# Another issue sequence for the 3155 pieces of a DeltaNet and FNet kernel on one core

## Chip, core and metric

One core of one Trainium2 chip runs the whole kernel. The metric is the device time of one launch in microseconds (us). The engines are PE (TensorE, matmuls), PEld (the same engine's weight loads), DVE (VectorE), ACT (ScalarE), POOL (GpSimd) and SP (SyncE, which starts most DMAs).

## What is computed

```python
batch, n_heads, seq, head_dim = (4, 8, 768, 48)
def _attn_ref(q, k, v, beta):
    k_n = k / (np.linalg.norm(k, axis=-1, keepdims=True) + 1e-06)
    state = np.zeros((B, H, D, D), dtype=np.float32)
    for t in range(S):
        kt, vt, bt = (k_n[:, :, t], v[:, :, t], beta[:, :, t, None])
        y[:, :, t] = np.einsum('bhd,bhde->bhe', q[:, :, t], state)
        v_old = np.einsum('bhde,bhd->bhe', state, kt)
        state = state + bt[:, :, :, None] * np.einsum('bhd,bhe->bhde', kt, vt - v_old)
    ...
def _moe_ref(x, w_ch1, w_ch2):          # x: (4, 768, 384), the heads side by side
    mixed = np.real(np.fft.fft(np.fft.fft(x, axis=1), axis=2)).astype(np.float32)
    u = x + mixed
    mu = np.mean(u, axis=-1, keepdims=True)
    var = np.mean((u - mu) ** 2, axis=-1, keepdims=True)
    un = (u - mu) / np.sqrt(var + 1e-06)
    ch = np.maximum(un @ w_ch1, 0.0) @ w_ch2      # 384 -> 1536 -> 384
    return (u + ch).astype(np.float32)
```

The two weight matrices come as 64-bit floats and are made into 32-bit floats on the chip.

## The kernel before

**How the work is cut.** The recurrence is done in chunks. Each of the four batches b has six blocks T of 128 positions, so there are 24 units u (six per batch), and each unit holds 8 heads in four pairs. For a unit the kernel loads q, k and v, normalises k, turns q and k by matmuls against the identity (`turn`: the matmuls are `tr`, L357, and two evictions of 128x256 follow, by `copy`), forms the products of keys with keys and with queries (`keys`, `gram`, whose masked evictions are L581 and L596), and inverts a triangular matrix for each head and chunk on DVE (`invert`, pairs of instructions L871 and L876; the first units go by `invert16`, which begins with two wide transposes, L701, and uses a triangle of ones made by the memsets L2087 and L2089). `join`, `blocks` and `quarters` build larger inverses from smaller ones, `chain0` and `step` carry the state through the chunks, and `outputs` writes the rows of x for the block.

**The second half.** When the six blocks of a batch are there, DVE folds x for the Fourier transform (`turns`, L1339), PE multiplies by the tables (`seq`, `half_axis`), and `feat` adds x and takes mean and variance (L1499 to L1512). `normed` then makes the normalised rows of one block: its `apply` (L1525, tile pm, for batch 0 always on DVE) writes 128x384 values, PE turns them (L357, `pp<-pack,pm`, three matmuls), and evictions bring them back as rows R. There are three groups g of two blocks T for each batch. For a group, `mlp` runs six slices of the first layer (`first(i)`, L354, `pp<-R,w`, 128x256, twelve matmul records in the trace) with relu evictions, each followed later by its slice of the second layer (`second(i)`, L354, `pp<-w,R`, 128x384, eight records). Only the first batch uses the plain form `mlp`; the weights that it needs are made ready in 18 slices, each by six operations: ACT (L1931), DVE (L1934), ACT (L1937), DVE (L1942), POOL's addition (L1947) and DVE (L1950).

**What sets the order.** Every piece of work is recorded by `P.op(engines, fn, ...)` and gets a number. Nothing is issued then. At the end `P.issue` walks the text `ORDER` (L58 to L138): two characters are a piece's number, one more names the engine where the piece allows several (most evictions allow DVE or ACT, memsets DVE or POOL), one more gives a PSUM bank for every new bank, and for a paced DMA of SP two more name the piece after which it may start. Every engine executes its pieces in just this order, and waits for data by semaphores that the framework puts in. A number past the last piece is a fill: `fill(kind, bank)` issues matmuls whose result nobody reads (kind 3 is a pair of 64x64 by 64x256, kind 4 one of 128x128 by 128x256, L2159; kind 0, at the start, many small ones, L2153).

Of the kernel before, what the change touches and what calls it, by code (L numbers as in the profile page):

```python
# [57 lines left out]
ATAAAMDAPBAODAHDAEBACBxTCARAKBAZAZAaAPAYAbGEABALBAXASANDAFBAeFCA9APAcCAdCAhDAAfBAgCAiAJDA7APA+APADBA  # L58
8AOAjAlxWGBPHEBQCAkAUFAmAtAVApAuCxAOBRCxVCBSGFBTCAGDA-CBBBCAIDBACBUCAvBCEHAxDFAAAyBDCAwBECBVBGBWAWA1
BcAzBZBkA0A2BFFCBXBGxWEA3xWEBvBaBwDgAiDOAmxWEBJxWEBKBbArBzBHxWEBYB0BIxWEB3AoBjB4BgAnBMAqxWExWEBOBNBe  # L60
A4B7BpBhBLxWEB8A5BlBdBmB-BnCAxWEBoCyADCDC0CIAAjBqH-H-DGCFCECHC6C6BrCIIBA6BxxWGDhEDCLDiBDjCC7BHC8CCMD
XDXC9CByCPxXGDICB1CQBfB2CTBiB5DYGDDPBHCUB6CXB9CYDQCB+CbDaCCzCxWFDHCH4BECBDRCCcCCH3BeCfCFDZCxWFCgC5C5
DDCCGxXBxXFxWFH5C+EBDbGHxWFCjxWFxWFCJCkC1CAC-CH7DcCC3CIoC0CKxWFIPB8xWFDdCCnDACxWExWGCNAsCpDJAHxXDxXF
IQA4CoBtIRCOxWEDLCDyC2CIIDZDKCxWEDzCD2CIHB+ESCRD3HxWFICEUCCSEWCEXAEVCD0CD4CDwByD1CIJCqETCDSHCD5ECrCV
EYCD6xWBCWD7IDCZEZFEaDND3CaxWDD8D9DkAEIYCkCdDTCIKILEbEcIXD0CeAQDDWCNxWBITxWBH6DlCDUCEAHChIED-CD+CxWC
xWFEDCEECECCEBCCiBuxWADmCIZClEdxWGEFDxWGCmDCDzEGCEHCEICEgHxWGBsEJCENABEKEDH8H9EkCCsCuCtH+EhCFqEjCE+x
WFxWFIxCrCvEPCEfBEiCELCxWFFrCFDHEOCIvIZFCBEeCFBCFECFvGFsBEMCFACIwECEQCHCE-CERCFuBIFIGGYCGWElDGXCFFHF
HDMGaCEwFtCFwCEpCIMGbFFxEEyCEnCEzCHHGHFBEoCGcBFGGZCEtAFCwHGCFyFIHDCEmCIyElGdBEqHDHICIzIbFzI1EvCDEBFJ
I5FGExGEEsCErBE0F0DqBF1I0I6EOFKCI7FwFMHEuCE1CC4FQCI8GZINGeF4DF3BFOCF7CE5E7BFLBHEBGfFPCF5CI2E2IOFNCI3
# [2123 lines left out]
```

The heart of `P.issue` is this:

```python
            i = take(2)
            if i >= len(self.ops):
                fill(i - len(self.ops), take(1))
                continue
            o, self.ins = self.ops[i], None
            e = o.engs[0] if len(o.engs) == 1 else ENGINES[take(1)]
            for b in o.new:
                b.slot = take(1)
            after = take(2) if o.kb and e == "SP" else i
            o.fn(e)
```

The eviction helper, whose lines the profile shows for three kinds of instruction, reads:

```python
    def copy(e, o, i, scale=None):
        if e == "ACT":
            I(nc.scalar.activation(o, i, ACT.Copy, **({} if scale is None else {"scale": scale})))   # L363
        elif scale is None:
            I(eng(e).tensor_copy(o, i))                                                              # L365
        else:
            I(eng(e).tensor_scalar(o, i, scale, None, op0=ALU.mult))                                 # L367
```

## Time and profile before

| | before |
|---|---|
| median of 3 runs | 624.71 us (624.24 to 625.9) |
| the profiled execution: its own time | 624.21 us |
| its span | 622.4 us |
| mean granted TensorE clock | 0.997 |
| PE busy | 606.6 us (97%) |
| DVE busy | 542.3 us (87%) |
| ACT busy | 292.6 us (47%) |
| POOL busy | 28.7 us (5%) |

A share of busy time is a mean over stages with different limits: the first 147 us (the first units, the weights, and batch 0 up to its layers) look otherwise than the rest, so the views below are cut by stage. In a view by windows a row gives the window, its length, then for PE, PEld, DVE, ACT and POOL the busy time with the number of instructions, the granted clock, the share of DMA time and GB/s. In a timeline a row gives start, duration, engine, line, operation, output and inputs, shapes and count, and in brackets how long the engine was idle before it and what ended that.

### The profile page before, as it was taken

The numbers are of one execution on the slowest core, as the hardware profiler recorded it, in microseconds if no ns is written. First come the engines' busy times: TensorE is split into PE (matmuls) and PEld (weight loads), VectorE is DVE, ScalarE is ACT, GpSimd is POOL, SyncE is SP. The second block draws the span as 40 slices with busy tenths as digits, with TensorE's granted clock in tenths as the row PEclk, the third lists the DMA queues.
The fourth block names the chain that finished last, engine by engine and source line by source line (L and its number), as shares of the span: only waits on it lengthen the run. The fifth ranks groups of instructions, "written<-read, shape, count | busy, mean of one in ns | idle before, by whom it ended". The sixth has DMA issues, their size and how long they took to land.

```text
span 622.4 us, 23113 instructions
## 1 busy us (share of the span) xinstructions
PE 606.6 (97%) x9870; PEld 529.8 (85%) x9870; DVE 542.3 (87%) x1631; ACT 292.6 (47%) x903; POOL 28.7 (5%) x36
## 2 busy tenths in 40 slices
PE   8998899999999999999999999999999999999997
PEld 8787888776778877999898978898889899999997
DVE  6999899999989889999777999999977898967574
ACT  6999757464255542725446435446731113332220
POOL 2022410110000000000000000000000000000000
PEclk9999989999999999999999999999999999999999
DMA  9546544520023200200220220110000000000010
GB/s 196 159 110 176 148 108 106 137 68 19 14 70 69 54 19 1 75 18 1 66 54 16 41 56 10 26 52 16 4 29 3 2 2 25 2 1 1 26 52 25
DMA packets 85443, 32.01 MB, mean 51 GB/s; under 512 B 75996, under 2 KB 80829, under 8 KB 85341
## 3 DMA queue, kind: packets, MB, share of 16 engines
q1 hardware_dynamic: 85149, 30.31, 19.7%
q8 instruction: 77, 1.26, 0.8%
q10 hardware_dynamic: 192, 0.23, 0.2%
q14 instruction: 25, 0.20, 0.1%
HBM read 25.82 MB, written 4.72 MB: 49 GB/s over the span
## 4 chain that ended last, share of the span: by engine, by line
PE 79%; DVE 15%; issue 2%; DMA 1%; ACT 1%; SPq 0%; DVEq 0%; ACTq 0%
PE pp L354 73%; PE pp L2159 3%; PE pp L357 3%; DVE R L1339 2%; DVE tmp L871 2%; DVE w L1950 1%; DVE rr L876 1%; DVE eo L1339 1%; ACT us L363 1%; DVE pm L1339 1%; PE pp L2153 1%; DVE us L581 1%; DMA x<-in_moe_w_ch_dram 1%; DMA us<-in_v_dram 1%; DVE w L1934 1%
## 5 line engine op out<-in xcount | busy, mean ns | idle before, releaser
L354 PE MATMUL pp<-R,w 128*128 128x256 f32 (+1 forms) x832 | 181.5, 367 | 0.7 <-DVE R L581 0.6
L354 PEld LDWEIGHTS pp<-R,w 128*128 128x128 f32 x832 | 144.6, 190 | 19.8 <-DVE R L581 0.9
L363 ACT ACTIVATE us<-pp 32x128 f32<-32x128 f32 (+3 forms) x211 | 68.3, 351 | 61.2 <-PE pp L354 43.7
L354 PE MATMUL pp<-w,R 128*128 128x384 f32 (+1 forms) x288 | 91.0, 440 | 0.7 <-DVE w L1950 0.7
L354 PEld LDWEIGHTS pp<-w,R 128*128 128x128 f32 x288 | 51.8, 190 | 22.7 <-DVE w L1950 1.3
L354 PE MATMUL pp<-us 64*64 64x64 f32 (+4 forms) x2560 | 62.8, 229 | 1.5 <-ACT us L363 0.5
L354 PEld LDWEIGHTS pp<-us 64*64 64x64 f32 (+2 forms) x2560 | 53.3, 131 | 6.2 <-ACT us L363 2.6
L871 DVE TENSOR_TENSOR tmp<-rr 128x30 f32<-128x30 f32 (+13 forms) x150 | 50.9, 343 | 2.5
L876 DVE TENSOR_TENSOR rr<-rr,tmp 128x168 f32<-128x168 f32 (+11 forms) x150 | 48.8, 328 | 2.6
L354 PE MATMUL pp<-u,us 64*48 64x48 f32 (+2 forms) x1360 | 41.9, 218 | 1.6 <-DVE u L365 0.8
L354 PEld LDWEIGHTS pp<-u,us 64*64 64x64 f32 (+1 forms) x1360 | 35.9, 131 | 7.8 <-issue 3.5
L363 ACT ACTIVATE R<-pp 128x384 f32<-128x384 f32 (+10 forms) x69 | 26.8, 404 | 29.2 <-PE pp L354 16.3
L1772 DVE TENSOR_TENSOR us<-us,pp 128x256 f32<-128x256 f32 x64 | 26.1, 416 | 12.5 <-ACT us L363 8.2
L363 ACT ACTIVATE x<-pp 64x192 f32<-64x192 f32 (+1 forms) x69 | 21.5, 324 | 32.0 <-DVE u L1248 21.8
L363 ACT ACTIVATE u<-pp 64x192 f32<-64x192 f32 (+1 forms) x65 | 21.2, 325 | 29.3 <-PE pp L354 26.6
L354 PE MATMUL pp<-st,us 48*64 48x48 f32 (+1 forms) x1104 | 27.1, 222 | 3.3 <-issue 3.0
L1593 ACT ACTIVATE R<-pp 128x512 f32<-128x512 f32 x24 | 14.3, 595 | 33.8 <-PE pp L354 33.5
L1808 ACT ACTIVATE R<-pp 128x512 f32<-128x512 f32 x21 | 12.5, 597 | 34.2 <-PE pp L354 29.3
L354 PEld LDWEIGHTS pp<-st,us 48*64 48x64 f32 x1104 | 22.3, 134 | 6.7 <-issue 4.1
L354 PE MATMUL pp<-R,ws 128*128 128x192 f32 x144 | 28.0, 327 | 0.0
L354 PE MATMUL pp<-us,gd 128*128 128x192 f32 x144 | 27.6, 327 | 0.0
L363 ACT ACTIVATE us<-us,nr 128x48 f32<-128x48 f32 x112 | 26.7, 330 | 0.2 <-DVE nr L678 0.2
(214 smaller groups left out, 1170.6 us busy)
## 6 DMA issues: line engine op xcount, KB each, us to landing
out_dram<-x SPq DMA_DIRECT2D x11, 384.0 KB
us<-in_k_dram SPq DMA_DIRECT2D x16, 192.0 KB
us<-in_q_dram SPq DMA_DIRECT2D x16, 192.0 KB
us<-in_v_dram SPq DMA_DIRECT2D x16, 192.0 KB
x<-in_moe_w_ch_dram SPq DMA_DIRECT2D x11, 242.0 KB
R<-in_moe_w_ch_dram SPq DMA_DIRECT2D x8, 256.0 KB
ws<-in_moe_w_ch_dram SPq DMA_DIRECT2D x5, 242.0 KB
us<-in_q_dram SPq DMA_DIRECT2D x6, 181.5 KB
```

What stands on the lines that cost most here:

```text
L354: I(nc.tensor.matmul(o, lhsT=lhsT, rhs=rhs, start=start, stop=stop, skip_group_check=True))
L357: I(nc.tensor.matmul(o, lhsT=src, rhs=ident[p0:p0 + n, p0:p0 + n], is_transpose=True, start=start, stop=True, skip_group_check=True))
L363: I(nc.scalar.activation(o, i, ACT.Copy, **({} if scale is None else {"scale": scale})))
L581: I(nc.vector.tensor_tensor(z.LT.rearrange(hs, s=2)[:, s], bk()[:, 0], m_su[:, None, :].broadcast_to([128, NJ, 64]), op=ALU.mult))
L871: I(eng(e).tensor_tensor(T_, R[:, :, j + 1:32, j:j + 1].broadcast_to([128, ns, n, j]), R[:, :, j:j + 1, 0:j].broadcast_to([128, ns, n, j]) ...
L876: I(eng(e).tensor_tensor(R[:, :, j + 1:32, 0:j], R[:, :, j + 1:32, 0:j], T_, op=ALU.add))
L1339: I(eng(e).tensor_tensor(o, i0, i1, op=op))
L1593: I(nc.scalar.activation(o, s, ACT.Relu))
L1772: vec(256, lambda e: I(nc.vector.tensor_tensor(o, i0(), i1(), op=ALU.add)), [], [aH] + list(wr), pr - P.ev, use=n)
L1808: I(nc.scalar.activation(o, s, ACT.Relu))
L1934: I(eng(e).tensor_scalar(cc, cc, LB, UB, op0=ALU.max, op1=ALU.min))
L2159: I(nc.tensor.matmul(pst[bank][x, 0:256], lhsT=w[x, 0:128 // tiles], rhs=w[x, 0:256], start=True, stop=True, skip_group_check=True))
```

## The change

Only the text `ORDER` differs. The same 3155 pieces stand in it, in another sequence, with 47 fills as before (kind 0 once, kind 3 forty times; of kind 4 there are six where there were five, and the one of kind 2 is gone). 370 of the 397 choices of PSUM banks differ, and 167 of the anchors of paced DMAs. Where a piece may run on several engines, the choice differs for some: DVE has 1648 pieces where it had 1612, ACT 773 where it had 806, POOL 29 where it had 32. The pieces of PE stand in nearly the same order, mostly no more than 8 places away. Two of the 81 rows of the table, by way of example:

```diff
 ORDER = """
-ATAAAMDAPBAODAHDAEBACBxTCARAKBAZAZAaAPAYAbGEABALBAXASANDAFBAeFCA9APAcCAdCAhDAAfBAgCAiAJDA7APA+APADBA
...
+AKDAODARAPBAMDxTCAAATAIBAEBAZAPACBAbDEAdBASAaAPAeBGABAcCAhACAfCA9APAGDAgBAiBPDEAjAkAlAmA7AEAtAWBRBAU
...
```

The first place is the start of DVE's list. The names us_75 to us_80 are the buffers of the first six units, pp_61 to pp_68 the eight PSUM banks, w_73 from L2089 the triangle of ones, gd and rr the matrices that `invert16` works on. Before:

```order
L485 MEMSET us_79 128x8x16 x2
L2087 MEMSET w_73 128x256
...
L2089 MEMSET w_73 128x15
L485 MEMSET us_76 128x8x16
L365 COPY us_76<-pp_66 128x4x64
L485 MEMSET us_75 128x8x16
L540 SCALAR_TENSOR_TENSOR gd<-pp_64,pack,gd 128x8x32
L540 SCALAR_TENSOR_TENSOR gd<-pp_61,pack,gd 128x8x32
L1996 COPY bcol<-pp_66 128x6x4x8
L701 STREAM_TRANSPOSE rr<-gd 128x1024
```

And after:

```order
L485 MEMSET us_75 128x8x16
L365 COPY us_75<-pp_65 128x4x64
L365 COPY us_76<-pp_67 128x4x64
L540 SCALAR_TENSOR_TENSOR gd<-pp_61,pack,gd 128x8x32
L540 SCALAR_TENSOR_TENSOR gd<-pp_63,pack,gd 128x8x32
L365 COPY us_79<-pp_65 128x4x64
L2087 MEMSET w_73 128x256
...
L2089 MEMSET w_73 128x15
L365 COPY us_79<-pp_64 128x4x64
L1996 COPY bcol<-pp_62 128x6x4x8
L706 STREAM_TRANSPOSE nr<-bcol 128x32
L701 STREAM_TRANSPOSE rr<-gd 128x1024
```

Three evictions of turns (rows 5, 9 and 26) came from ACT to DVE, ahead of the first wide transpose L701, and the triangle moved from ahead of the first eviction to behind the keys' evictions L540.

The second place is DVE around the last of the two instructions L1525 of batch 0's second group, whose outputs PE turns (mv_110 is block T2, mv_111 block T3). Before, T3 comes at row 365 and T2, the later one, here:

```order
L1950 SCALAR_TENSOR_TENSOR w_73<-x_97,w_73 128x512
L871 TENSOR_TENSOR tmp<-rr 128x240
L876 TENSOR_TENSOR rr<-rr,tmp 128x15x16
L660 STREAM_TRANSPOSE nr<-bcol 128x32
L1512 RECIPROCAL mv_110<-mv_110 128x1
L1525 TENSOR_SCALAR pm_99<-x_96,mv_110 128x384
L871 TENSOR_TENSOR tmp<-rr 128x238
L876 TENSOR_TENSOR rr<-rr,tmp 128x14x17
L1950 SCALAR_TENSOR_TENSOR w_73<-ws,w_73 128x512
```

After, T2 comes at row 340 and T3, now the later one, here:

```order
L1950 SCALAR_TENSOR_TENSOR w_73<-x_97,w_73 128x512
L365 COPY R_98<-pp_64 128x512
L1503 BN_AGGR mv_112<-mv_112 128x2
L876 TENSOR_TENSOR rr<-rr,tmp 128x14x17
L871 TENSOR_TENSOR tmp<-rr 128x234
L365 COPY us_80<-pp_65 128x512
L876 TENSOR_TENSOR rr<-rr,tmp 128x13x18
L871 TENSOR_TENSOR tmp<-rr 128x228
L1525 TENSOR_SCALAR pm_99<-x_96,mv_111 128x384
L1950 SCALAR_TENSOR_TENSOR w_73<-ws,w_73 128x512
```

The later of the two stands 24 rows further down DVE's list, 399 where it was 375; the weights' step L1950 that followed it at a distance of three rows follows it at once.

The third place is PE where those transposes stand; rows that only repeat with other banks are left out. `pp<-pack,pm` are the transposes of a block, `pp<-R_81,w_72` a first layer, `pp<-w_73,R_81` a second layer, and the rows 64x2x64 the products of `gram`. Before, around the later block T2 (rows 1020 to 1060 of PE's list):

```order
L357 MATMUL pp_61<-pack,pm_99 128x128 x3
L354 MATMUL pp_68<-w_73,R_81 128x384
...
L354 MATMUL pp_64<-us_80 64x2x64
...
L354 MATMUL pp_63<-us_79 64x2x64
...
L354 MATMUL pp_67<-R_81,w_72 128x256 x6
L354 MATMUL pp_68<-w_73,R_81 128x384 x2
```

After, around the later block T3 (rows 1023 to 1063):

```order
L357 MATMUL pp_63<-pack,pm_99 128x128 x3
L354 MATMUL pp_61<-w_73,R_81 128x384
...
L354 MATMUL pp_65<-R_81,w_72 128x256 x6
...
L354 MATMUL pp_63<-us_80 64x2x64
...
L354 MATMUL pp_67<-us_79 64x2x64
...
L354 MATMUL pp_61<-w_73,R_81 128x384 x2
```

Behind the later block's transposes stand the same pieces, a second layer, two grams and the first layer of the new group, but the first layer now comes ahead of the grams.

160 lines of the change are left out of this document (80 added, 80 removed).

## The prediction

> **What bounds the kernel now.** I read the page first, then the engines' busy time by stage, then the timelines of PE and DVE where one stage hands over to the next, and last the waits of PE. The page's busy times, DVE's and ACT's 40 slices, and the chain that ended last:
>
> ```profile
> PE 606.6 (97%) x9870; PEld 529.8 (85%) x9870; DVE 542.3 (87%) x1631; ACT 292.6 (47%) x903; POOL 28.7 (5%) x36
> DVE  6999899999989889999777999999977898967574
> ACT  6999757464255542725446435446731113332220
> PE 79%; DVE 15%; issue 2%; DMA 1%; ACT 1%; SPq 0%; DVEq 0%; ACTq 0%
> ```
>
> PE holds 79% of the chain and DVE 15%. But DVE's digits are at 8 and 9 through the first third and ACT's only in the second to fourth slice, so the beginning has a limit of its own. The windows by stage show it; the last two rows cut the span in two:
>
> ```profile
> 0.00:8.90 8.90, 7.50 (x135) 6.71 (x136) 3.00 (x27) 3.82 (x10) 3.85 (x16) 1.00 0.88 179
> 8.90:42.00 33.10, 32.50 (x734) 25.62 (x735) 32.27 (x113) 31.78 (x105) 2.80 (x2) 1.00 0.59 154
> 42.00:87.00 45.00, 39.98 (x1387) 37.23 (x1385) 42.37 (x118) 34.50 (x113) 12.24 (x9) 0.96 0.55 143
> 87.00:106.00 19.00, 18.06 (x224) 16.62 (x223) 18.59 (x54) 13.59 (x43) 2.64 (x2) 1.00 0.45 109
> 106.00:137.74 31.74, 31.60 (x243) 24.34 (x241) 30.71 (x80) 17.40 (x42) 5.29 (x4) 1.00 0.43 105
> 147.30:500.00 352.70, 350.61 (x6223) 299.00 (x6223) 315.73 (x933) 159.51 (x504) 0.62 (x2) 1.00 0.13 31
> 0.00:147.30 147.30, 137.68 (x2799) 116.25 (x2799) 136.14 (x411) 104.79 (x320) 28.12 (x34) 0.99 0.52 128
> 147.30:622.40 475.10, 468.88 (x7073) 413.53 (x7072) 406.18 (x1221) 187.85 (x583) 0.62 (x2) 1.00 0.11 28
> ```
>
> From 8.9 to 137.74 us DVE is idle for 0.83, 2.63, 0.41 and 1.03 us (window less busy time), 4.90 in all: it is full. PE looks just as full there, but part of its work is fills, which nobody waits for. From 147.3 on PE is busy 350.61 of 352.70 us and DVE has 37 us of room. So work added to DVE ahead of 138 us moves the end, and work added behind 147 us doesn't. The handover shows in PE's timeline and, below it, in DVE's; the last two rows are POOL's:
>
> ```profile
> 137.89 0.52 PE L357 MATMUL pp<-pack,pm 128*128 128x128 f32 x3 [0.29 <-DVE pm L1525]
> 139.16 2.85 PE L354 MATMUL pp<-w,R 128*128 128x384 f32 x8 [0.75 <-DVE w L1950]
> 144.53 2.86 PE L354 MATMUL pp<-R,w 128*128 128x256 f32 x12 [0.61 <-DVE R L581]
> ...
> 131.50 1.39 DVE L871 TENSOR_TENSOR tmp<-rr 128x240 f32<-128x240 f32 x1
> 132.81 1.44 DVE L1525 TENSOR_SCALAR pm<-x,mv 128x384 f32<-128x384 f32 x1
> 136.22 0.40 DVE L871 TENSOR_TENSOR tmp<-rr 128x240 f32<-128x240 f32 x1
> 137.26 0.48 DVE L1525 TENSOR_SCALAR pm<-x,mv 128x384 f32<-128x384 f32 x1
> 138.42 0.69 DVE L1950 SCALAR_TENSOR_TENSOR w<-ws,w 128x512 int32<-128x512 int32 x1
> ...
> 131.28 1.34 POOL L1947 TENSOR_TENSOR w<-w,x 128x512 int32<-128x512 int32 x1 [14.00 <-DVE w L1942]
> 132.58 1.46 POOL L1947 TENSOR_TENSOR w<-w,ws 128x512 int32<-128x512 int32 x1
> ```
>
> PE's transposes start 0.15 us after the later L1525 (137.26 + 0.48 = 137.74), PE having been idle for 0.29 us. All that PE does in the next ten microseconds waits for DVE three times, 1.65 us in sum. I call the end of the later L1525 of this group the gate.
>
> **The change part by part.**
>
> *More rows on DVE ahead of the gate.* The gate is row 375 of DVE's list before and row 399 after: 24 instructions more, nearly all evictions that were ACT's. The price of one: the first five windows up to the gate hold 3.00 + 32.27 + 42.37 + 18.59 + 30.71 = 126.94 us in 27 + 113 + 118 + 54 + 80 = 392 instructions, counting the row 0 to 8.9, so 0.324 us. 24 x 0.324 = +7.8 us. The eviction itself costs more on DVE, so that 24 x 0.42 = +10.1 is the other end:
>
> ```profile
> L365 DVE COPY us<-pp 128x256 f32<-128x256 f32 x2 | 0.8, 421 | 3.4 <-PE pp L357 3.4
> L363 ACT ACTIVATE us<-pp 128x256 f32<-128x256 f32 x34 | 11.0, 402 | 3.1 <-PE pp L357 2.4 <-PE pp L354 0.6
> ```
>
> I take 7.8, since some of the new rows are small memsets and reciprocals.
>
> *The triangle moved behind the first evictions.* Its 16 memsets now lie in a time in which DVE is idle anyway:
>
> ```profile
> 1.69 0.27 DVE L2087 MEMSET w<- 128x256 f32 x1
> 2.03 0.29 DVE L2089 MEMSET w<- 128x1 f32 x15
> 5.84 0.42 DVE L365 COPY us<-pp 128x256 f32<-128x256 f32 x1 [3.38 <-PE pp L357]
> 8.01 0.88 DVE L540 SCALAR_TENSOR_TENSOR gd<-pp,pack,gd 128x256 f32<-128x256 f32 x2 [1.60 <-ACT gd L363]
> ```
>
> The 3.38 us ahead of the first eviction wait for PE's first turn, and no eviction can use them; the triangle could, and is taken out of them: +0.6 us (0.27 + 0.29, rounded up). Ends: 0, if DVE finds a later hole for it, and 0.6.
>
> *What takes the new work up.* DVE's hole of 1.60 us ahead of L540 is where the evictions at rows 5 and 6 now stand: 1.6 us, all of it used. The later holes sum to 4.90 us. They end on PE and ACT, and ACT's list is 29 rows shorter, so its results come earlier; ends 0 and 4.90, and I take half, 2.45. The gate then moves by 7.8 + 0.6 - 1.6 - 2.45 = +4.35 us, between +1.9 (all holes used) and +9.1 (24 dear evictions, no later hole used: 10.1 + 0.6 - 1.6).
>
> *Behind the gate.* PE was only 0.29 us ahead of DVE there, so PE follows the gate. Of the two waits behind it, the one on L1950 (0.75) shrinks, since that step stands one row behind the gate: L1950 then ends 0.69 us after the gate where PE, with its transposes, is ready after 0.15 + 0.52, and 0.1 is left. The one on the gram's eviction L581 (0.61) can go, since the first layer now comes ahead of the grams. -0.65 - 0.61 = -1.26; ends -1.36 and 0. The front: 4.35 - 1.26 = +3.1 us.
>
> *After 147 us.* PE's pieces are the same, in nearly the same order; other banks, anchors and engines set small waits. The longest waits of PE from 147.3 us on:
>
> ```profile
> PE pp L354 <- issue: 0.9, 1, 0.9
> PE pp L354 <- DVE st L1277: 0.4, 1, 0.4
> PE pp L354 <- DVE R L1339: 0.3, 1, 0.3
> PE pp L354 <- ACT us L363: 0.2, 1, 0.2
> ```
>
> Those on DVE and ACT sum to 0.9, and I let all three go: -0.9 us. The upper end of a gain is PE's whole idle time there, 475.10 - 468.88 = 6.22 us; on the other side new waits of the same size, +0.9. DMAs have room (share 0.11), POOL has two instructions there, and SP's queue is paced by anchors whose pieces come at nearly the same time: nothing for these. The fills number 47 before and after, so PE's own work is the same.
>
> *Sum.* 3.1 - 0.9 = +2.2 us. Against the profiled execution's 624.21 us (span 622.4 and 1.8 around it) that is 626.4; the median of the runs, 624.71, stands 0.5 above it, and the forecast for a median is 626.9 us.
>
> **The rivals.** A measurement of this kernel can tell about 0.3%, 1.9 us, from no change.
>
> *Faster: ACT, not DVE, comes last in the beginning.* From 8.9 to 42 us ACT is busy 31.78 of 33.10 us, as full as DVE, and the state chain of batch 0, which follows up to 87 us, waits for evictions of both: PE is idle for 45.00 - 39.98 = 5.02 us there. With ACT relieved and two engines at work on the first turns, that idle time could go, in part. Were four of the five microseconds gained, with the -0.9 after 147 us unchanged and the gate no later, the time is 624.7 - 4.0 - 0.9 = 619.8. It decides if DVE's list isn't what the gate follows: DVE would have to have finished it before 137 us, with 24 rows more. Against it: DVE's 4.90 us of holes are fewer than the 7.8 us of new rows.
>
> *Same: the holes take it all.* With all 4.90 us used the gate moves by +1.9; 1.9 - 1.26 - 0.9 = -0.3, and the time is 624.4. For it: ACT's rows that DVE waits for come earlier. Against it: holes that wait for PE's own order stay.
>
> *Slower still: DVE held while POOL adds, and the clock.* L871 took 1.39 us and L1525 1.44 us in the time of POOL's two additions, where the same instructions took 0.40 and 0.48 at 136.22 and 137.26 us: 1.0 us for each one caught. There are 18 additions, before as after, but other instructions stand next to them. Two more caught cost +2.0 us, two fewer gain as much. [...]
>
> A longer wait of PE at a gate can also cost clock, as these two windows show:
>
> ```profile
> 76.00:80.00 4.00, 1.97 (x98) 1.83 (x92) 4.00 (x12) 1.22 (x5) 0.18 (x1) 1.00 0.37 95
> 80.00:84.00 4.00, 4.00 (x83) 3.76 (x83) 3.76 (x9) 1.80 (x6) 1.28 (x1) 0.57 0.38 109
> ```
>
> PE idle for 2.03 us of four, then the granted clock at 0.57 for the next four: 4 x 0.43 = 1.7 us of work lost. If PE waits for DVE in one more place as long, that is +1.7 us. The Trainium skill, page "TensorE: Matmul & The Clock Gate", Part 1, states a window of about 3.4 us of idleness before the clock halves; here half of one four-microsecond window sufficed. Both together: 626.9 + 2.0 + 1.7 = 630.6.
>
> **How the numbers follow.** My forecast, the front later by 2 to 5 us and a small gain behind: 0.33. Slower still: 0.10. Same: 0.27. Faster: 0.30, not less, because the holes of DVE and ACT alternate in the beginning, and the sum of one engine's list can't show whether the waits between the two shrink. So slower by over 0.3%: 0.43, within 0.3%: 0.27, faster: 0.30. The range reaches from 619.5, the faster case with 0.3 to spare, to 632: the gate's upper end, +9.1, with the 1.26 and the 0.9 off, gives 624.7 + 6.9 = 631.6. About 2 in 10 lie outside. The forecast's own range is 625.5 to 630 (the gate at +2.5 to +6.5, the rest as in the sum).
>
> **What would show it.** In the profile after, I look for: the later L1525 of batch 0's second group ending at 142.1 us (137.74 + 4.35) with DVE's idle time up to there down by about 4; PE's transposes of pm right after it; the second layer behind waiting 0.1 us for L1950 and no wait on L581; the PE position that stood at 147.3 us at about 150.4; from there to the end 474 us (475.10 before). It would be wrong if the gate ended before 138.5 us: then ACT was the limit, or DVE's evictions are shorter beside a relieved ACT. It would also be wrong if the rest behind 150 us differed from 474 by over 2 us: then waits too short for the view of waits decide, of which I have a sum, 6.22 us, and not the causes. If the gate is late and PE's beginning isn't, PE's order around it has more room than 0.29 us.

## The result: 3.5% slower, and the profile after

| | before | after |
|---|---|---|
| median | 624.48 us (624.24 to 625.9, 4 runs) | 646.54 us (646.2 to 647.4, 4 runs) |
| ratio | | 1.035 [1.0331, 1.0369] |
| span of the profiled execution | 622.4 us | 644.4 us |
| mean granted clock | 0.997 | 0.984 |

The forecast was 626.9 us. The measured 646.54 us lie 14.5 us above the range's upper end of 632; the change costs 22 us. The page of the changed kernel, in the rows shown of before and the granted clock's 40 slices:

```profile
PE 613.6 (95%) x9870; PEld 533.2 (83%) x9870; DVE 556.8 (86%) x1667; ACT 281.9 (44%) x863; POOL 29.0 (4%) x33
DVE  5889989999998779999976899999986798887573
ACT  4578865714237653252544443364642112332220
PEclk9799999999999989999999999999999999999999
PE 66%; DVE 27%; issue 4%; ACT 2%; DVEq 0%; ACTq 0%
```

PE's share of the chain is 66% where it was 79%, DVE's 27% where it was 15%. DVE is busy 14.5 us longer, ACT 10.7 us less, but PE too is busy 7.0 us longer with the same 9870 matmuls, and two slices of its clock (the second, and the fifteenth, from 225.5 us) lie below 9. The windows say where. In the first fence, of the kernel after, the last two rows cut the span at the gate, which is now at 153.17 us; the second has the same two rows of before, whose gate was at 137.74:

```profile
0.00:8.90 8.90, 7.50 (x144) 6.72 (x146) 2.88 (x10) 3.90 (x10) 3.39 (x13) 1.00 0.87 180
8.90:42.00 33.10, 25.59 (x456) 20.11 (x456) 29.18 (x117) 18.85 (x63) 0.00 (x0) 0.79 0.48 121
42.00:87.00 45.00, 39.29 (x1303) 34.53 (x1298) 40.36 (x116) 36.17 (x113) 10.19 (x8) 1.00 0.52 136
0.00:153.17 153.17, 133.53 (x2711) 112.49 (x2711) 137.06 (x412) 93.19 (x276) 27.06 (x30) 0.96 0.47 118
153.17:644.40 491.23, 480.06 (x7159) 420.73 (x7159) 419.73 (x1256) 188.67 (x588) 1.91 (x3) 0.99 0.12 28
```

```profile
0.00:137.74 137.74, 129.63 (x2711) 110.53 (x2711) 126.92 (x388) 101.09 (x307) 26.84 (x33) 0.99 0.54 134
137.74:622.40 484.66, 476.93 (x7159) 419.25 (x7159) 415.39 (x1245) 191.55 (x597) 1.91 (x3) 1.00 0.11 28
```

The matmul counts of the two parts are the same (2711 and 7159), so the cut is at the same work. 15.4 of the 22 us lie ahead of the gate: DVE is busy 10.1 us longer there (137.06 against 126.92) and idle 5.3 us longer (153.17 - 137.06 = 16.1 against 10.8). Behind it 6.6 us are lost: PE is busy 3.1 us longer with the same work, and idle 3.4 us longer.

The row from 8.9 to 42 us is the new thing. Before, PE, DVE and ACT were all full there. Now PE is idle for 7.5 us (0.6 before), ACT for 14.2 (1.3), DVE for 3.9 (0.8), and the granted clock is 0.79. In the same time PE starts 456 matmuls where it started 734. The timelines of after in this stretch show it, PE's rows that wait and one of the fills first, then DVE's, then ACT's:

```profile
13.14 1.26 PE L354 MATMUL pp<-us 48*64 48x64 f32 x66 [2.12 <-DVE us L365]
15.74 1.02 PE L354 MATMUL pp<-us 48*64 48x64 f32 x27 [1.34 <-DVE us L365]
16.65 5.87 PE L2159 MATMUL pp<-pack 64*64 64x256 f32 x31
27.44 0.71 PE L357 MATMUL pp<-pack,us 64*128 64x64 f32 x16 [2.67 <-DVE us L365]
28.97 1.14 PE L354 MATMUL pp<-us 48*64 48x64 f32 x32 [0.82 <-DVE us L365]
...
10.06 1.88 DVE L701 STREAM_TRANSPOSE rr<-gd 128x1024 f32<-128x1024 f32 x1
12.72 1.02 DVE L365 COPY us<-pp 128x256 f32<-128x256 f32 x3
14.39 0.88 DVE L540 SCALAR_TENSOR_TENSOR gd<-pp,pack,gd 128x256 f32<-128x256 f32 x2 [0.39 <-ACT gd L363]
17.43 0.88 DVE L540 SCALAR_TENSOR_TENSOR gd<-pp,pack,gd 128x256 f32<-128x256 f32 x2 [0.86 <-ACT gd L363]
18.32 0.19 DVE L761 TENSOR_TENSOR tmp<-w 128x28 f32<-128x28 f32 x1
26.63 0.75 DVE L365 COPY us<-pp 128x256 f32<-128x256 f32 x2
...
13.89 0.84 ACT L363 ACTIVATE gd<-pp,pack 128x256 f32<-128x256 f32 x2 [1.30 <-PE pp L354]
16.93 0.84 ACT L363 ACTIVATE gd<-pp,pack 128x256 f32<-128x256 f32 x2 [2.20 <-PE pp L354]
```

The evictions of turns that came to DVE stand in its list behind the wide transpose L701 (10.06 to 11.94 us) and L725. PE waits 2.12 us for them; ACT, which evicts what PE then computes, waits 1.30 for PE; DVE's L540 waits 0.39 for ACT; then the round goes once more, with 1.34, 2.20 and 0.86. It is a ring of three engines, and no one of them is busy all the time. The first step of the inversion, L761, starts at 18.32 us; before it stood here, in DVE's timeline of before:

```profile
13.30 0.17 DVE L761 TENSOR_TENSOR tmp<-w 128x28 f32<-128x28 f32 x1
```

That was 5.0 us earlier. At 26.63 two evictions stand behind the inversion's own rows, and PE waits 2.67 us for them. What the waits do to the clock, in windows of after:

```profile
12.00:16.00 4.00, 1.52 (x74) 1.38 (x78) 3.57 (x12) 1.39 (x4) 0.00 (x0) 0.80 0.35 83
16.00:20.00 4.00, 4.00 (x47) 3.95 (x45) 2.97 (x14) 3.07 (x12) 0.00 (x0) 0.50 0.25 50
28.00:32.00 4.00, 3.18 (x49) 2.63 (x46) 3.88 (x21) 3.16 (x9) 0.00 (x0) 0.50 0.15 40
32.00:36.00 4.00, 4.00 (x58) 2.28 (x59) 3.97 (x16) 1.02 (x4) 0.00 (x0) 0.64 0.88 273
```

Before, the clock was 1.00 in all of these windows. So 31 fill matmuls take 5.87 us in after, 189 ns each, where before took 4.48 us for 39 of them, 115 ns each, as PE's timeline of before has it:

```profile
12.90 4.48 PE L2159 MATMUL pp<-pack 64*64 64x256 f32 x39
```

The second place with a low clock is at 220 us, in the steady part. PE's timeline of after, then its windows, then the row of before that answers to the third:

```profile
221.69 0.32 PE L354 MATMUL pp<-u,us 64*64 64x48 f32 x3 [1.26 <-issue]
225.52 4.76 PE L354 MATMUL pp<-R,w 128*128 128x256 f32 x12
...
220.00:224.00 4.00, 2.74 (x115) 2.52 (x111) 2.35 (x9) 1.99 (x8) 0.00 (x0) 0.82 0.50 100
224.00:228.00 4.00, 4.00 (x42) 3.45 (x35) 3.37 (x9) 3.38 (x14) 0.31 (x1) 0.50 0.02 4
228.00:232.00 4.00, 4.00 (x115) 3.24 (x115) 1.91 (x6) 1.25 (x4) 0.00 (x0) 0.82 0.00 0
```

```profile
208.35 2.86 PE L354 MATMUL pp<-R,w 128*128 128x256 f32 x12
```

PE stops for 1.26 us within one row of equal matmuls, with no engine named, and the twelve matmuls of a first layer that follow take 4.76 us where they took 2.86.

**Where PE falls behind.** From here on "late" means: the start of a piece of PE in one profile less the start of the same piece in the profile of before, as a median over the pieces that before starts within a few microseconds. After is 0.4 to 1.0 us early up to 8 us and 2.0 late at 12; the pieces from 17 to 20 us stand in another order and are 4 to 13 late; it is 11 to 13 at 23 to 25 us and 12.5 at 45, then between 10 and 14 up to 120 us; 14.9 at 200, 18.9 at 213 (the stop above), 19.2 at 240, 20.9 from 248, 22 to 23.6 from 350 on. Three rows that are easily found show the same: batch 0's first product with the tables, batch 1's and batch 3's, in PE's timeline of before and, below, of after:

```profile
93.94 2.85 PE L354 MATMUL pp<-tab,R 128*97 128x193 f32 x16 [0.72 <-DVE R L1339]
247.65 5.11 PE L354 MATMUL pp<-tab,R 128*96 128x65 f32 x48
515.73 5.11 PE L354 MATMUL pp<-tab,R 128*96 128x65 f32 x48 [0.34 <-DVE R L1339]
```

```profile
106.37 2.85 PE L354 MATMUL pp<-tab,R 128*97 128x193 f32 x16 [1.27 <-DVE R L1339]
268.53 5.11 PE L354 MATMUL pp<-tab,R 128*96 128x65 f32 x48 [1.62 <-DVE R L1339]
537.90 5.06 PE L354 MATMUL pp<-tab,R 128*96 128x65 f32 x48
```

Late by 12.4, 20.9 and 22.2 us. So of the 15.4 us at the gate, of which the prediction speaks, 12.4 are there at batch 0's row already, and nearly all of these at 45 us; the other 3.0 arise between this row and the gate.

### The profile page after: what moved, and what is told of

Read it like the earlier page. It is cut to its first block, busy times and chain, and to the rows that moved or that the text cites. A ratio compares the mean times of both kernels' runs of the same rounds, so it can differ in the third digit from the quotient of the medians.

```text
span 644.4 us, 23117 instructions
## 1 busy us (share of the span) xinstructions
PE 613.6 (95%) x9870; PEld 533.2 (83%) x9870; DVE 556.8 (86%) x1667; ACT 281.9 (44%) x863; POOL 29.0 (4%) x33
## 3 DMA queue, kind: packets, MB, share of 16 engines
q1 hardware_dynamic: 85149, 30.31, 18.9%
q8 instruction: 77, 1.26, 0.8%
## 4 chain that ended last, share of the span: by engine, by line
PE 66%; DVE 27%; issue 4%; ACT 2%; DVEq 0%; ACTq 0%
PE pp L354 62%; DVE rr L876 3%; DVE tmp L871 3%; DVE R L1339 2%; PE pp L357 2%; PE pp L2159 2%; DVE pm L1339 1%; DVE w L1950 1%; DVE x L1314 1%; DVE eo L1339 1%; DVE rr L670 1%; ACT us L363 1%; DVE R L1656 1%; DVE gd L604 1%; DVE us L581 1%
## 5 line engine op out<-in xcount | busy, mean ns | idle before, releaser
L354 PEld LDWEIGHTS pp<-R,w 128*128 128x128 f32 x832 | 146.2, 192 | 19.4 <-ACT us L363 0.4
L363 ACT ACTIVATE us<-pp 32x128 f32<-32x128 f32 (+3 forms) x187 | 62.0, 347 | 83.3 <-PE pp L354 57.7
L354 PE MATMUL pp<-us 64*64 64x64 f32 (+4 forms) x2560 | 64.8, 234 | 7.2 <-DVE us L365 4.3
L354 PEld LDWEIGHTS pp<-us 64*64 64x64 f32 (+2 forms) x2560 | 54.8, 135 | 12.3 <-DVE us L365 4.7
L876 DVE TENSOR_TENSOR rr<-rr,tmp 128x228 f32<-128x228 f32 (+10 forms) x150 | 51.1, 344 | 3.0
L871 DVE TENSOR_TENSOR tmp<-rr 128x210 f32<-128x210 f32 (+10 forms) x150 | 49.1, 329 | 2.4
L363 ACT ACTIVATE R<-pp 128x384 f32<-128x384 f32 (+10 forms) x72 | 26.3, 394 | 33.7 <-PE pp L354 17.1
L363 ACT ACTIVATE u<-pp 64x192 f32<-64x192 f32 (+1 forms) x65 | 21.1, 325 | 30.2 <-PE pp L354 28.7
L363 ACT ACTIVATE x<-pp 64x192 f32<-64x192 f32 (+1 forms) x70 | 22.0, 324 | 22.6 <-PE pp L354 12.3
L1808 ACT ACTIVATE R<-pp 128x512 f32<-128x512 f32 x23 | 13.7, 596 | 38.7 <-PE pp L354 34.5
L2159 PE MATMUL pp<-pack 64*64 64x256 f32 (+1 forms) x172 | 29.3, 434 | 0.8 <-DVE us L365 0.8
L1248 DVE TENSOR_TENSOR u<-u,pp 64x192 f32<-64x192 f32 x66 | 21.9, 348 | 5.9 <-PE pp L354 4.7
L354 PE MATMUL pp<-tab,R 128*96 128x128 f32 (+9 forms) x192 | 23.8, 281 | 2.9 <-DVE R L1339 2.9
```

The source lines that it names most:

```text
L354: I(nc.tensor.matmul(o, lhsT=lhsT, rhs=rhs, start=start, stop=stop, skip_group_check=True))
L871: I(eng(e).tensor_tensor(T_, R[:, :, j + 1:32, j:j + 1].broadcast_to([128, ns, n, j]), R[:, :, j:j + 1, 0:j].broadcast_to([128, ns, n, j]) ...
L876: I(eng(e).tensor_tensor(R[:, :, j + 1:32, 0:j], R[:, :, j + 1:32, 0:j], T_, op=ALU.add))
L1248: I(nc.vector.tensor_tensor(U[:, s], U[:, s], psum(b1[s])[a, s0:s1].rearrange("p (j d) -> p j d", d=D), op=ALU.subtract))
L1808: I(nc.scalar.activation(o, s, ACT.Relu))
L2159: I(nc.tensor.matmul(pst[bank][x, 0:256], lhsT=w[x, 0:128 // tiles], rhs=w[x, 0:256], start=True, stop=True, skip_group_check=True))
```

## The experiments

Each kernel is given with its ratio to the kernel before on the same chip, whose median lay between 625.3 and 626.7 us (624.5 for after); "loss" is the difference of these two medians, 22.1 us for after. The ratio comes with its interval from the runs and isn't exactly the quotient of the two medians. The lateness at the three rows above and at the end (span less 622.4) comes from its one profile:

| kernel | median us | loss us | ratio | at batch 0's row | batch 1's | batch 3's | end |
|---|---|---|---|---|---|---|---|
| after | 646.54 | 22.1 | 1.035 [1.0331, 1.0369] | 12.4 | 20.9 | 22.2 | 22.0 |
| before's list up to 13 us | 638.31 | 11.7 | 1.0192 [1.016, 1.0224] | 7.4 | 12.5 | 13.5 | 13.6 |
| up to 30 us | 637.82 | 11.2 | 1.0182 [1.0139, 1.0225] | 7.2 | 12.9 | 13.5 | 13.7 |
| up to 56 us | 630.54 | 4.4 | 1.008 [1.0051, 1.0109] | 4.8 | 11.1 | 11.6 | 11.4 |
| up to 100 us | 632.58 | 7.3 | 1.0105 [1.0074, 1.0135] | 3.4 | 8.5 | 9.4 | 9.2 |
| up to 182 us | 635.16 | 9.1 | 1.0132 [1.0096, 1.0168] | 3.6 | 8.5 | 11.1 | 11.0 |
| up to 269 us | 637.62 | 12.1 | 1.0167 [1.0121, 1.0213] | 1.5 | 3.1 | 17.4 | 17.6 |
| after's list up to 100 us, then before's | 645.73 | 20.4 | 1.0293 [1.0245, 1.034] | 15.6 | 23.9 | 22.3 | 22.3 |
| after, eleven evictions on ACT | 647.11 | 21.0 | 1.0342 [1.0283, 1.0401] | 13.9 | 18.6 | 22.7 | 22.5 |
| after, nine evictions on ACT | 643.11 | 17.6 | 1.0277 [1.0232, 1.0322] | 11.1 | 16.7 | 18.6 | 18.7 |
| after, inversion steps ahead | 643.91 | 18.4 | 1.0282 [1.0244, 1.032] | 13.2 | 18.6 | 19.9 | 19.8 |
| after, both and one more | 641.86 | 15.2 | 1.0254 [1.021, 1.0298] | 9.8 | 13.9 | 16.1 | 16.2 |
| control: before, one pair of fills more | 625.0 | -1.1 | 0.9979 [0.9956, 1.0002] | 3.4 | 3.4 | 1.9 | 1.9 |

The profile of the 56 us kernel comes from an execution of 635.6 us, five above its median, so its lateness is read with care.

### Which part of the list

Each of these lists is before's up to one piece of PE, with everything that stands ahead of it, and after's from there on (one the other way round); every piece takes the engine, bank and anchor of the list it comes from, save for one to three banks in the lists cut at 13, 56 and 182 us. Fills stand at other places in the two lists, so that those cut at 13, 30 and 56 us have 50, 53 and 49 of them instead of 47. The first of them against the changed kernel, its first row of ORDER by way of example:

```diff
 ORDER = """
-AKDAODARAPBAMDxTCAAATAIBAEBAZAPACBAbDEAdBASAaAPAeBGABAcCAhACAfCA9APAGDAgBAiBPDEAjAkAlAmA7AEAtAWBRBAU
+ATAAAMDAPBAODAHDAEBACBxTCARAKBAZAZAaAPAYAbGEABALBAXASANDAFBAeFCA9APAcCAdCAhDAAfBAgCAiAJDA7APA+APADBA
...
```

**Before up to 100 us, then after.**

> The first 110 pieces of PE (to 100 us in before) and all that stands ahead of them in before's order, then the rest in after's order, each with its own engines, banks and anchors. Theory 'beginning': the 12.3 us by which after is late at 140 us all arise ahead of the cut and are carried unchanged to the end, so this kernel runs in 646.5 - 12.3 = 634 us (+10 over before). Rival 'whole order': the later losses (4 us at 208 us, 2 us at 250 us) are consequences of the late beginning and go with it: 625 to 628 us. Rival 'rest': the beginning is cheap to repeat and the loss comes back behind the cut: 640 us or more.

632.58 us, a loss of 7.3: two thirds of the 22 come with the list ahead of 100 us. In the profiles 9.0 us of this are there at batch 0's row (3.4 us late against 12.4). The 7.3 are what after's list costs behind it, with the seam. This profile is already 6 us late right behind batch 0's row, in a beginning that is instruction for instruction before's; its stops on "issue" of 1.46, 1.20 and 1.75 us are part of that. A single lateness is therefore good to some 3 us.

**After up to 100 us, then before.**

> The counterpart: after's order up to its 110th piece of PE, then before's. Theory 'beginning': 624.5 + 12.3 = 637 us. Rival 'whole order' (the later losses follow from the late beginning): 643 to 647 us. Rival 'rest': below 631 us.

645.73 us. PE is late by 15 us at 90 us, the seam at 100 to 120 us adds 8 (a list cut there isn't tuned to itself: PE waits 2.11 us for an eviction of ACT, and the clock falls to 0.5), and from there on before's list adds nothing: 23.9 at batch 1's row, 22.3 at the end. The total alone would have misled here.

**Before up to 13 us (14 pieces of PE), and up to 30 us (24 pieces).**

> Before's order up to PE's 14th piece (13 us in before, 17 us in after), then after's. Theory 'first round': after lets DVE evict the second round's keys ahead of the first round's inversion, which starts at 18.3 us where it started at 13.3; that and the cooling behind it is the cause of the late beginning, so most of the 12 us comes back: 634 to 638 us. Rival 'later': the lateness arises behind 17 us again: 643 to 647 us.

> The same with the cut at PE's 24th piece (30 us in before). Both theories: as with the cut at 100 us, 631 to 635 us, if nothing of the lateness arises between 30 and 100 us; rival: above 638 us, if the order from 30 to 60 us has its own losses.

638.31 and 637.82 us, losses of 11.7 and 11.2. With the first 13 us put back, sequence and engines (13 pieces run on another engine than in after), 10 us of the 22 are gone. In the profile 5.0 us are there at batch 0's row (7.4 us late against 12.4); another 3.4 come between it and batch 1's, where after has its stop at 220 us. The next 17 us give nothing more.

**Before up to 56 us (60 pieces), and up to 182 us (160 pieces).**

> Before's order up to PE's 60th piece (56 us in before), then after's. With the cut at 30 us this gave 637.8, with the cut at 100 us 632.6. Theory 'second place' (after's order from 30 to 56 us costs 4 us by itself): 632 to 634 us. Rival: 636 to 639 us, if the loss arises from 56 to 100 us.

> Before's order up to PE's 160th piece (182 us in before), then after's. With the cut at 100 us: 632.6. Theory 'gate' (the rest of the loss is DVE's late second group and the waits up to 160 us): 626 to 629 us. Rival 'later' (the waits at the folds of batch 1 and behind): 630 to 633 us.

630.54 and 635.16 us, losses of 4.4 and 9.1. The cut at 56 us wins another 7, those at 100 and 182 us win nothing beyond it. A seam costs something of its own (in the last, some 3 us from 188 us on, with new waits of 0.80 and 0.99 us), so the cuts tell the beginning from the rest, and within the rest no more than that.

**Before up to 269 us (250 pieces).**

> Before's order up to PE's 250th piece (269 us in before), then after's. Theory: of the loss behind 100 us (some 7 us with the cut there) most arises from 180 to 269 us, so 626 to 628 us are left. Rival: it arises behind, 630 us or more.

637.62 us, and inconclusive: at this cut 88 of the bank choices don't fit together and had to be given anew. It is 3.1 us late up to 280 us and falls back by another 14 after that (its profile comes from an execution of 641.7 us, four above its median). What part of that the new banks cost isn't shown, so it doesn't say where after loses.

### The engines or the sequence

**After's sequence with before's engines, and before's sequence with after's engines.** A piece of an example row, the eviction of a turn:

```diff
 # after's sequence, before's engine for each piece
-L365 COPY us_79<-pp_65 128x4x64         (DVE)
+L363 ACTIVATE us_79<-pp_65 128x4x64     (ACT)
```

> After's sequence, banks and anchors, but every piece on the engine that it had in before. Theory 'DVE's list' (the prediction's own: the evictions moved to DVE make it late): DVE loses about 24 instructions ahead of the gate, and 8 to 12 us come back: 634 to 638 us. Rival 'sequence' (the pieces stand in a bad sequence, whatever the engine): 643 to 648 us.

> Before's sequence, banks and anchors, with after's engines. Theory 'DVE's list': DVE, full ahead of 138 us, has 8 to 10 us more to do there: 632 to 636 us. Rival 'sequence': the engines alone cost little: 624 to 628 us.

667.04 us, 1.0654 [1.0597, 1.071], and 669.42 us, 1.0689 [1.0646, 1.0731]. Neither theory had this: each half of the change by itself costs 41.7 to 44.1 us, twice what both cost together. PE's waits, as the view of waits has them for the second (microseconds in total, times, longest):

```profile
PE pp L354 <- DVE u L365: 6.9, 3, 3.5
PE pp L354 <- ACT u L363: 3.9, 4, 2.8
PE pp L357 <- DVE us L365: 3.5, 2, 2.0
```

On engines that work in order, a row's place says when it can run only together with the rows ahead of it on the same engine. A list with other engines is another list, so "engines" and "sequence" aren't two terms that can be added.

### The start on DVE

**Eleven evictions of the first 31 us back on ACT.** The rows against after, on DVE (all appear on ACT as L363):

```diff
-L365 COPY us_75<-pp_65 128x4x64
-L365 COPY us_76<-pp_67 128x4x64
-L365 COPY us_79<-pp_65 128x4x64
 ...
-L365 COPY us_76<-pp_67 128x4x64
```

> After's order with the eleven turn evictions of its first 31 us that it moved to DVE back on ACT, as in before. Theory 'DVE's list' (the prediction's term): DVE has 11 x 0.4 = 4.4 us less ahead of the inversions, PE's waits for DVE's evictions of 2.1, 1.3 and 2.7 us go: late by 5 to 7 us instead of 12.5 at 45 us, 636 to 641 us. Rival 'sequence': the same eviction waits on ACT, 644 to 648 us.

647.11 us, 1.0342 [1.0283, 1.0401], a loss of 21.0: no gain that can be told, with 11 x 0.42 = 4.6 us of rows taken off DVE ahead of the gate. Up to the gate, which ends at 154.79 us here, DVE is busy 2.5 us less than in after and idle 4.1 us longer. PE now waits for ACT at the very start, in its timeline:

```profile
7.41 1.99 PE L354 MATMUL pp<-us 48*64 48x64 f32 x64 [1.70 <-ACT us L363]
```

**Nine of them, without the two of the first units.**

```diff
 L365 COPY us_75<-pp_65 128x4x64
 L365 COPY us_76<-pp_67 128x4x64
 ...
-L365 COPY us_79<-pp_65 128x4x64
 ...
-L365 COPY us_76<-pp_67 128x4x64
```

> After's order with nine turn evictions of the second and third rounds back on ACT, but the two of the first round (u0 and u1, second bank) left on DVE, since putting those back too made the start 3 us late. Theory 'DVE's list': DVE has 9 x 0.4 = 3.6 us less ahead of the inversions and the start stays early: late by 6 to 8 us at 45 us instead of 12.5, 638 to 643 us. Rival 'sequence': 645 to 648 us.

643.11 us, 1.0277 [1.0232, 1.0322], a loss of 17.6, 4.5 less than after's. The waits of 2.12 and 1.34 us become 1.00 (on ACT) and 0.65, that of 2.67 becomes 0.91 and 1.44. At batch 0's row PE is 1.3 us less late than in after, and the gate ends 1.3 us earlier, at 151.84 us. The time lies at the upper end of what 'DVE's list' gave, so this kernel doesn't speak for the sequence against it.

**The first round's inversion steps ahead of the second round's key evictions**, engines as in after:

```diff
-L540 SCALAR_TENSOR_TENSOR gd<-pp_68,pack,gd 128x8x32
-L540 SCALAR_TENSOR_TENSOR gd<-pp_62,pack,gd 128x8x32
...
 L761 TENSOR_TENSOR tmp<-w_73 128x28
+L540 SCALAR_TENSOR_TENSOR gd<-pp_68,pack,gd 128x8x32
 L767 TENSOR_TENSOR w_73<-w_73,tmp 128x2x14
+L540 SCALAR_TENSOR_TENSOR gd<-pp_62,pack,gd 128x8x32
```

> After's order with ten pieces of DVE put earlier and nothing else changed: the last turn eviction of the second round, and the first round's scaling and first inversion steps, ahead of or between the evictions of the second round's keys, as in before. Theory 'sequence' (these evictions wait for ACT and PE, 0.39 and 0.86 us, and PE for them, while the first round's inversion stands behind them): the inversion starts 3 us earlier, and 3 to 8 us come back with the clock: 638 to 643 us. Rival 'DVE's list' (the same sum of work in another order): 645 to 648 us.

643.91 us, 1.0282 [1.0244, 1.032], a loss of 18.4, 3.7 less than after's. L761 starts at 16.00 us instead of 18.32, and DVE no longer stands still before a key eviction while inversion rows wait behind it. But the gain doesn't last: PE is some 1.7 us less late than in after at 24 to 45 us, but no longer from 60 us on. At batch 0's row it is 13.2 us late, where after is 12.4, and the gate ends at 153.92 us, 0.75 later than in after. It is ahead again only behind 220 us, where the stop on "issue" lasts 0.94 us and the clock stays at 1.00. So these 3.7 us don't show that the ring at the start costs time.

**Both, and one more eviction right behind its turn.**

```diff
+L365 COPY us_80<-pp_61 128x4x64
...
-L365 COPY us_80<-pp_61 128x4x64
-L365 COPY us_78<-pp_68 128x4x64
```

> After's order with the three single edits together: nine turn evictions back on ACT, the first round's inversion ahead, and the one remaining late turn eviction put behind its turn. Theory: the single gains (3.4 and 2.6 us, and 2 to 4 for the third) add up, PE stays warm, the beginning is late by 4 to 6 us instead of 12.5 at 45 us: 636 to 639 us, as with before's first 30 us (637.8). Rival: they overlap, 640 to 643 us.

641.86 us, 1.0254 [1.021, 1.0298], a loss of 15.2: 6.9 less than after's, where 4.5 + 3.7 = 8.2 would be the sum of the first two. The 1.3 us between them lie inside this kernel's interval, so whether the gains add up or overlap isn't shown. PE is 9.0 us late at 45 us, 12.5 in after; 2.5 us are won at batch 0's row, and the gate ends at 150.74 us, 2.4 earlier than in after.

**Only the evictions that PE waits for 2.67 us, put right behind their turns.**

```diff
+L365 COPY us_77<-pp_65 128x4x64
+L365 COPY us_80<-pp_61 128x4x64
 L741 STREAM_TRANSPOSE nr<-nr 128x32
 L485 MEMSET us_79 128x8x16
+L365 COPY us_78<-pp_68 128x4x64
...
-L365 COPY us_80<-pp_61 128x4x64
-L365 COPY us_78<-pp_68 128x4x64
...
-L365 COPY us_77<-pp_65 128x4x64
```

> After's order with three turn evictions of the third round (L365) put on DVE right behind their turns instead of 3 us later, behind the first round's inversion steps; nothing else. Theory 'sequence': PE waited 2.67 us at 24.8 us for one of them; that wait shrinks, PE cools less, and 2 to 4 us come back: 642 to 645 us. Rival 'DVE's list' (DVE has the same to do, and the inversions come that much later): 645 to 648 us.

649.63 us, 1.0368 [1.0314, 1.0422], a loss of 23.0: no gain. The wait did shrink, to 0.70 us, and the next one took its place, in PE's timeline of this kernel:

```profile
26.78 0.71 PE L357 MATMUL pp<-pack,us 64*128 64x64 f32 x16 [0.70 <-DVE us L365]
30.13 0.69 PE L357 MATMUL pp<-pack,us 64*128 64x64 f32 x8 [2.01 <-DVE us L485]
```

L485 is a memset of 0.17 us that clears a unit's padding, which depends on nothing. In after it stands at 28.47 us on DVE behind the inversion's rows, the last of five such between 12.6 and 28.5 us; before had all of them done by 6.4 us, in time that DVE and POOL had to spare.

### The unread matmuls and the clock

**Before without the ten pairs of fills at 13 to 17 us.**

```diff
 L354 MATMUL pp_63<-us_78 64x64
-L2159 MATMUL pp_65<-pack 64x256 x20
 L357 MATMUL pp_61<-pack,us_75 128x64
```

> Before's order without the ten fills that PE runs from 13.1 to 17.3 us. Theory 'clock': PE idles four microseconds, the clock halves, and the slow pieces behind make the beginning late: 628 to 633 us. Rival 'DVE's order': DVE sets the pace there and the fills only stand beside it: 624 to 626 us.

633.74 us, 1.0124 [1.0089, 1.016]: work that nobody reads, taken away, makes the kernel 7 us slower. PE's timeline and its window:

```profile
16.19 0.79 PE L357 MATMUL pp<-pack,us 64*128 64x64 f32 x9 [3.00 <-ACT us L363]
...
16.00:20.00 4.00, 3.18 (x34) 2.12 (x36) 4.00 (x14) 3.05 (x11) 0.00 (x0) 0.50 0.72 188
```

PE would have waited there anyway; the fills spent that wait. Without them the clock halves. Only 2.0 us of lateness are there at 20 to 45 us, though; it is 4.5 at 100 us, 7.0 at 240 and 8.8 at the end, with a stop on "issue" of 1.40 us at 309 us. How the rest follows from the first is not shown.

**After without the eight pairs of fills at 16.7 to 22.5 us.**

```diff
 L354 MATMUL pp_65<-us_78 64x64
-L2159 MATMUL pp_67<-pack 64x256 x2
-L2159 MATMUL pp_64<-pack 64x256 x2
-L2159 MATMUL pp_67<-pack 64x256 x12
 L357 MATMUL pp_65<-pack,us_77 128x64
```

> After's order without the eight fills that PE runs at half clock from 16.7 to 22.5 us. Theory 'fills on the path': PE's next turns come up to 5 us earlier, and 2 to 5 us come back: 641 to 644 us. Rival 'DVE': PE waits for DVE's evictions right behind them anyway, 645 to 648 us; and if the clock then stays low longer, 648 us or more.

650.33 us, 1.0384 [1.0341, 1.0426], a loss of 24.8, 2.7 more than after's, though the two intervals overlap: the clock stays at 0.50 from 16 to 32 us. Slow as they are in after, nothing is won by leaving the fills out.

**After with 16 more pairs of fills ahead of the four waiting pieces.**

```diff
 L357 MATMUL pp_64<-pack,us_78 128x64
+L2159 MATMUL pp_67<-pack 64x256 x10
 L354 MATMUL pp_68<-us_80 64x64
```

> After's order with 16 more unread matmul pieces, five, three, six and two, just ahead of the four pieces of PE at which PE waited 2.12, 1.34, 2.67 and 0.82 us for DVE's evictions between 11 and 29 us; they fill the waits and change nothing else. Theory 'clock' (the waits halve TensorE's clock from 14 to 24 and from 28 to 36 us, and the slow matmuls, fills among them, then lie on the path): the clock stays at 1.0 there, PE is late by 6 to 9 us instead of 12 at 45 us, and the time is 638 to 643 us. Rival 'DVE's order': PE waits for DVE whatever its clock, 645 to 648 us.

661.12 us, 1.0569 [1.0525, 1.0612]. The design failed. The fills waited themselves, for the eviction of the bank they write to:

```profile
14.32 4.11 PE L2159 MATMUL pp<-pack 64*64 64x256 f32 x18 [2.78 <-DVE us L365]
```

A kernel like after but with a warm clock there wasn't had in this way, and it wasn't tried in another, so what the clock alone costs isn't shown.

**A control: before with one pair of fills more behind the ten.**

```diff
-L2159 MATMUL pp_65<-pack 64x256 x20
+L2159 MATMUL pp_65<-pack 64x256 x22
```

> Before's order with one more unread matmul piece (0.43 us) behind the ten that run from 13.1 to 17.3 us: a measure of how far the time answers to any small shift. Theory 'causes': 624 to 627 us. Rival 'fetch' (waits of PE on nothing that the profile shows, and the halved clock after them, fall elsewhere with every shift): 627 to 635 us, with other such waits.

625.0 us, 0.9979 [0.9956, 1.0002]: no difference that can be told. But PE's stops on "issue" from 42 to 90 us are not those of before. The view of waits, of this kernel and then of before:

```profile
PE pp L354 <- issue: 6.9, 6, 2.9
```

```profile
PE pp L354 <- issue: 2.5, 3, 2.0
```

It is 3.4 us late at 100 us and 1.9 at the end. So such stops come and go, and a lateness of 2 to 3 us in one profile says nothing about a list. What they are the traces show by their times: each of the 132 stops on "issue" of PE in the twenty traces here ends 1.1 to 1.7 us after a packet of 16 KB has landed on the DMA queue q8, which the page calls "instruction" (the control's longest, of 2.86 us, ends at 82.02 us, its packet landed at 80.53). There are 77 such packets, one for 256 of the 19740 matmuls and weight loads. So the rival 'fetch' had the nature of the stops right, though not a price of them: PE waits for its next instructions. No run changed the fetching, so this rests on the times alone.

## Why the prediction was wrong

**"What takes the new work up" is the step that failed.** It let the holes of DVE shrink by 4.05 us (1.6 + 2.45), on the ground that they end on PE and ACT and that ACT has fewer rows. They grew by 5.3: 3.1 from 8.9 to 42 us and 2.0 from 42 to 87. ACT's results came no earlier, since ACT waits for PE, which waits for DVE. The difference, 9.3 us, is most of what the gate missed (+15.4 against +4.35). The profile of before is an early one, though. In the control and in the kernels cut at 182 and 269 us, which have before's list up to the gate (the control with one pair of fills more), the gate ends at 140.9 to 141.4 us, and DVE is idle for 13.6 to 15.0 us up to it instead of 10.8. Against these the holes grew by 1.1 to 2.5 us. They shrank in no comparison.

**"More rows on DVE ahead of the gate"** gave +7.8, with +10.1 as its other end; DVE is busy 10.1 us longer. As a count it held. As a cause it is a small part: with nine of these rows back on ACT the gate ends 1.3 us earlier, with eleven 1.6 us later, and the time stays 1.034. What the sum has no term for is the beginning. That the first 13 us of the list bear a large part of the loss is shown: put back, they take 10 us off the time and 5.0 off the lateness at batch 0's row. The sequence counts there at the same number of rows: this kernel and the one with nine evictions on ACT both have 403 instructions of DVE up to the gate, which ends at 148.17 us in the one and at 151.84 in the other (one profile each). That it is the order of the first forty rows, in which the evictions for PE stand behind a transpose of 1.88 us and behind inversion rows, is argued from the waits. The edits that change this order bring 1.3 us at batch 0's row (nine evictions), nothing (inversion steps ahead) and 2.5 (both, with one more), so about half of the 5.0 us stays open.

At the gate itself the forecast was nearer. Between batch 0's row and the transposes behind the gate, after falls back by 3.0 us, and so, by 3.0 to 3.2, do all ten other kernels that have after's list there and pass the row at full clock, while the control and the kernel cut at 182 us lose nothing. The prediction had +4.35 for the gate.

**"Behind the gate"** was right in its parts. PE's transposes start 0.15 us after the gate as before, though the profile puts the end of their wait to an eviction of ACT, which was done at 153.31 us, 0.14 behind L1525. The second layer follows them without a wait for L1950 and there is none on L581, in PE's timeline of after:

```profile
153.32 0.52 PE L357 MATMUL pp<-pack,pm 128*128 128x128 f32 x3 [0.67 <-ACT lo L363]
153.82 2.85 PE L354 MATMUL pp<-w,R 128*128 128x384 f32 x8
```

**"After 147 us", -0.9 with 6.2 as the bound of the unknown**, missed too: +6.6 behind the gate. About 4 us of it are the stop at 220 us and the 3.4 us of clock after it (4 us windows at 0.82, 0.50 and 0.82). Another 1.6 are the wait for L1339 at batch 1's row, where before has none. The four kernels that are before's up to 13, 30, 56 or 100 us and after's from there all have this wait. They lose 5.1 to 6.3 us between batch 0's row and batch 1's, but 3.0 to 4.8 of that ahead of the gate and only 0.4 to 3.3 behind it. Their clock is at 1.00 from 216 to 236 us; in the one cut at 56 us a stop of 1.29 us ahead of 234.94 us is followed by 0.57 from 236 to 240. Between the two rows the control lost nothing and the kernel without the ten fills 4.2, so part of this may be scatter. Which rows of after's list bring it isn't settled.

**The rivals.** "Faster" (ACT last) and "same" (the holes take it all) rested on the same step and fell with it. "Slower still" had the clock as one of its two mechanisms, and that is what happened, but priced as one drop of 1.7 us. The windows from 12 to 36 us fall short of full speed by 6.8 us in sum, and PE is idle 6.9 us longer from 8.9 to 42 us. By PE's busy time in each of these windows the shortfall is 5.9 us, and with the 6.9 that makes 12.8, about the 12.5 us at 45 us; the fall of the clock follows the waits, so the two aren't independent. The other mechanism, DVE held while POOL adds, is absent at L1525, where both take 0.47 us, and falls on other rows: L876 took 1.33 us at 138.90 us while POOL added from 138.73 to 140.02, and PE then waited 1.32 us for DVE at 142.02. In sum it changed little: up to the gate 12 instructions of DVE, 10 in before, stand more than 0.2 us above the usual time of their form (the lower quartile over the traces), by 10.9 and 9.1 us.

**On the clock's rule.** The prediction set a page of the Trainium skill beside its price of a drop: "TensorE: Matmul & The Clock Gate", Part 1, with a window of about 3.4 us of idleness before the clock halves. The runs here differ in size. The stop at 220 us lasted 1.26 us, with work on either side, and the clock was 0.50 four microseconds later; the same followed two waits of 2.12 and 1.34 us with 1.26 us of work between them. The same part of the Trainium skill says that a free-running window of activity sets the clock, and with that the trace agrees better: of the four microseconds from 12 to 16 us PE was busy for 1.52. No length of a single stop divides the cases, though: before's own stop of 2.03 us ahead of 78.5 us was followed by a clock of 0.57, and in the control a stop of 2.86 us ahead of 82 us by 1.00, in the four microseconds around it and in the next eight. Nor does PE's busy time in such a window: it was 2.74 us of four ahead of the fall at 224 us and 1.98 in the control without one.

The step to do otherwise: the profile of before had the ring in plain sight. PE, DVE and ACT were all full from 8.9 to 42 us, which I read as "DVE is full" and priced as DVE's rows. Three full engines in a stretch where each waits for the next leave no room for a row that moves; its cost isn't its duration, but how long the next engine waits for it.

## What to carry to other kernels

Where three in-order engines hand work round in a ring, don't sum the rows of the fullest: follow one piece round, and for each row that moves ask which engine waits for its result and what now stands ahead of it. Keep short rows that depend on nothing (paddings, constants) in the idle microseconds at the start (no run here moved these alone), and keep unread matmuls where PE waits: ten pairs of them were worth 7 us here. To find where a reordered list loses, cut it: one list up to a piece, the other from there on; read the lateness of the pieces, not the total, know the scatter by a control first, and don't split engines from sequence, as each alone cost over 40 us here.

## What the runs showed of the hardware

- A stop of PE on "issue", in the middle of equal small matmuls, of 0.2 to 2.9 us, ends 1.1 to 1.7 us after a 16 KB packet of instructions has landed, in all 132 cases. The stops differ between lists with nearly the same beginning (2.5 us in three of them from 42 to 90 us in before, 6.9 us in six in the control). The control's 6.9 us left it 1.9 us late at the end; the one of 1.26 us at 220 us was followed by a halved clock and made after 4 us later.
- The clock halved after a single stop of 1.26 us and after one of 1.29 (in the list cut at 56 us), and after 3.46 us of waits in two parts within 4.7 us; it stayed up through one of 1.37 us (after without its eight fills, ahead of 232.82 us) and one of 2.86.
- A matmul whose result nobody reads needs a PSUM bank all the same, and waited 2.78 us for that bank's eviction.
